# Retention with two expert layers on one core: weight loads spread over the attention chunks, and one more row buffer

## The chip, the cores and the metric

The kernel runs on one core of one Trainium2 chip. The time is the device time of one execution in microseconds (us); lower is better. The engines are TensorE (PE), VectorE (DVE), ScalarE (ACT), GpSimd (POOL) and SyncE (SP); SP, ACT and POOL each issue DMAs in their own order.

## What is computed

Four batches of 576 positions, eight heads of 64, go through retention (attention with a decay instead of a softmax). The 2304 rows of 512 go to one of eight experts each, and then through a layer that takes the maximum of three products.

```python
def _attn_ref(q, k, v):
    scores = scale * np.matmul(q, k.transpose(0, 1, 3, 2))
    gamma = 1.0 - 2.0 ** (-5.0 - np.arange(H, dtype=np.float32))
    rel = pos[:, None] - pos[None, :]
    Dmat = np.where(rel >= 0, gamma[:, None, None] ** rel[None, :, :], 0.0)
    return np.matmul(scores * Dmat[None, :, :, :], v)

def _moe_ref(x, w_gate, w1, w2, capacity):
    logits = x @ w_gate
    expert_idx = np.argmax(logits, axis=1)
    ...
    h = np.maximum(np.einsum('ecd,edf->ecf', disp, w1), 0.0)   # 8 x [512, 1024]
    y = np.einsum('ecf,efd->ecd', h, w2)                       # 8 x [1024, 512]
    ...                                                        # row i: gate_w[i] * y[its expert, its place]

def _moe2_ref(x, w1, w2, w3, w_out):
    h = np.maximum(np.maximum(x @ w1, x @ w2), x @ w3)
    return h @ w_out
```

All arrays are float32 (the last layer's weights are float64 in the input and are decoded in the kernel).

## The kernel before, in words

**Order.** The order on each engine is the order of the program. Engines wait for each other where tiles are written and read; a tile's buffer is given to a new tile when the old one's last reader is done. DMAs of SP and ACT stand in the queue of the engine that issues them, and an issue that has to wait stops what is queued behind it.

**Attention.** The loop runs over 20 chunks t of 128 rows (every fifth has 64). In the turn of chunk t, PE does the scores of chunk t+1 (L270), the transposes of chunk t-1 (L491), the update of the decayed state (L295) and the outputs of chunk t (L315, L327). DVE masks the scores (cut, L276), scales the outputs (L336) and the values (vprime, L254), and does the gate. Loads of qk run five chunks ahead and those of kv up to six; qk has five buffers and kv six. The table otab, with which DVE scales the outputs, is made in the first four turns: a spread multiplies the decay table decs by a selector and puts it on 128 partitions (L664).

**The gate** works on groups: chunks 0 to 4, 5 to 9 and 10 to 13. For a chunk in a group, take reduces the logits on DVE (L382), and then ACT copies the transposed rows from PSUM to a buffer xg (L389); the next transposes write the same PSUM tile. One turn after a group's last chunk, group_choose picks the experts (L408 to L415, gives goh); in the turn after that group_place counts on PE (gpo, L433, read by DVE at L443 as ghit), group_weigh finds weights and places, and group_send scales two chunks' rows a turn and stores them from xg to xd in HBM (L483, L484). Chunks from 14 on are done one by one by gate1 (L344 to L365), position (on PE, L497, into the same PSUM tile as gpo) and gate2. In chunk 18 POOL gathers the first expert's rows from xd (L174). The rows of the last three chunks are first set to zero in xd (L728) and added on PE.

**Weights of the experts.** Each expert has eight units of 128 x 1024 (four of w1, four of w2). load_unit brings one from HBM to raw (three buffers, SP). A split makes two parts of it: split_hi on ACT rounds it (L144), split_lo on DVE takes the rest (L149); split_lo frees raw. Units 0 to 7 have homes that are there from the start, those after them homes that come with the experts. In the attention loop units are loaded at LOAD_AT and split at SPLIT_AT, the DVE half one turn later, each followed there by another load; after the loop next_split splits one unit and loads the next.

**Experts.** Expert e does mm1 in eight steps f (a<-xt,w), each followed by ACT and DVE making h (L1113, L1114), and mm2 in four steps d (b<-h,w), each followed by ACT's copy to y (L1144). next_split stands after some steps. The last layer follows from some 420 us on and is not touched.

The names of the change: LOAD_AT, SPLIT_AT, ZERO_AT, the number of xg buffers, spread_otab with its selector sel, next_split's places in mm1 and mm2, and next_load.

Of the kernel before, what the change touches and what calls it, by code (L numbers as in the profile page):

```python
# [8 lines left out]
F32 = mybir.dt.float32  # L9
# [11 lines left out]
P = 128  # L21
B, H, S, D = 4, 8, 576, 64
DM = H * D
# [27 lines left out]
NPATCH = 3  # L51
LOAD_AT = [2, 4, 5]
SPLIT_AT = [4, 6, 7, 8, 9]
EARLY_SCATTER = 10
# [24 lines left out]
def retention_moe_max3_kernel(ctx: ExitStack, tc: tile.TileContext, qk, kv, consts, decay, tokid, cap, wg, wts, wts2, out):  # L79
# [81 lines left out]
    def next_load():  # L161
        if nxt["load"] < NUNIT:
            load_unit(nxt["load"])
            nxt["load"] += 1
# [33 lines left out]
    def attention():  # L198
        with ExitStack() as c2:
# [141 lines left out]
            def gate1(t):  # L341
# [25 lines left out]
                if NCHUNK - NPATCH <= t < NCHUNK - 1:  # L367
                    xg_t[t] = wk.tile([P, DM], F32, tag="xg", name=f"xg{t}", bufs=7)
                    act.activation(
                        out=xg_t[t][:L].rearrange("p (c n) -> p c n", c=NC), in_=xps_t[t][:L, :, :P], func=AF.Copy  # L370
                    )
# [7 lines left out]
            def take(t):  # L379
                L = CHUNKS[t][2]  # L380
                i = GROUP_OF[t]
                dve.tensor_reduce(  # L382
                    out=lgs[i % 2][:L, t - GROUPS[i][0]],
                    in_=xps_t[t][:L, :, P:].rearrange("p c e -> p e c"),
                    axis=AX.X,
                    op=ALU.add,
                )
                xg_t[t] = wk.tile([P, DM], F32, tag="xg", name=f"xg{t}", bufs=7)
                act.activation(  # L389
                    out=xg_t[t][:L].rearrange("p (c n) -> p c n", c=NC), in_=xps_t.pop(t)[:L, :, :P], func=AF.Copy  # L390
                )
# [114 lines left out]
            def gate2(t):  # L506
# [12 lines left out]
                xps = xps_t.pop(t)[:L, :, :P]  # L519
                xg = xg_t.pop(t) if t in xg_t else wk.tile([P, DM], F32, tag="xg", name=f"xg{t}", bufs=7)  # L520
                if t < NCHUNK - NPATCH:
# [135 lines left out]
            decs = st.tile([H, S], F32, name="decs")  # L657
            sel = st.tile([H, NPAIR, 2, D], F32, name="sel")

            def spread_otab(j):  # L660
                a, n = j * P, min(P, S - j * P)
                bank = ps_1.tile([P, DM], F32, tag="po", name=f"spread{j}")
                for r in range(NPAIR):
                    pe.matmul(  # L664
                        bank[:, r * n : (r + 1) * n], lhsT=sel[:, r].rearrange("h a d -> h (a d)"),
                        rhs=decs[:, a : a + n], start=True, stop=True,
                    )
                act.activation(
# [20 lines left out]
            for s_ in state:  # L689
# [11 lines left out]
            vprime(1)  # L701
            act.activation(
                out=sel,
                in_=ident[:H, :H].rearrange("h (r a) -> h r a", a=2).unsqueeze(3).to_broadcast([H, NPAIR, 2, D]),
                func=AF.Copy,
            )
            spread_otab(0)
# [9 lines left out]
            for t in range(NCHUNK):  # L717
# [3 lines left out]
                if t == 0:  # L721
                    act.dma_start(out=who_d.rearrange("(p c) o -> p (c o)", p=P), in_=zero)
                if t == 4:
                    tail = sum(L for _, _, L in CHUNKS[NCHUNK - NPATCH :])
# [73 lines left out]
                if t - 1 in SPLIT_AT:  # L798
                    split_lo(nxt["split"] - 1, dve)
                    if nxt["load"] < 8:  # L800
                        next_load()
                if t < NPOS - 1:
# [139 lines left out]
    with tc.manual_schedule():  # L942
# [158 lines left out]
        def mm1(e):  # L1101
            xt, wide = xt_t.pop(e), WIDTH[e]
            for f in range(F // P):
# [15 lines left out]
                if f % 2:  # L1119
                    units.pop(8 * e + f // 2)  # L1120
                if f % 2 or (e in (1, 3, 4) and f == 4):
                    if (e, f) != (0, 1):
                        next_split()
                dec_step(e, f)

        def mm2(e):
# [3 lines left out]
            for d in range(NC):  # L1130
# [14 lines left out]
                if e == E - 1:  # L1145
                    ysplit_part(0, d)
                next_split()
                dec_step(e, F // P + d)
# [70 lines left out]
        dec_load(1)  # L1219
        find_order()  # L1220
        load_x(1)
        for c in range(NC // 2):
# [559 lines left out]
```

## Time and profile before

| | |
|---|---|
| median of 3 runs | 668.2 us (661.24 to 670.61) |
| profiled execution | 665.12 us, its span 663.1 us |
| PE busy in the span | 634.7 us (96%) |
| DVE, ACT, POOL busy | 440.1, 277.2, 215.5 us |
| mean granted clock of PE | 0.984 |
| DMA | 124.05 MB, mean 187 GB/s |

Busy time of PE is that of matmuls, which are pipelined. The granted clock is a share of the full 2.4 GHz; 0.50 is 1.2 GHz. The idle time of an engine that nothing waits for costs nothing.

### The profile page before, as it was taken

Reading aid. Unit: us, or ns where it says so; the run is one execution under the profiler, and the core shown is the slowest. Engines: PE = TensorE matmul, PEld = TensorE weight load, DVE = VectorE, ACT = ScalarE, POOL = GpSimd, SP = SyncE. Lnnn points to the kernel's source line nnn. Section 1 sums busy time; section 2 is a strip of 40 time slices with the busy share of each in tenths; the row PEclk is TensorE's granted clock in tenths of the full one; section 3 lists DMA queues with packets and bytes.
Section 4 is the critical chain, followed back from the end, with each engine's and each line's share of the span. In section 5 each row is a group of like instructions: output and inputs, shape, how many; then the busy total and the mean of one; then the engine's idle time right before and its main releaser. Section 6 shows DMA issues by size and latency. Waiting matters only on the chain. (4 is left out here: it accounts for less than half of the span.)

```text
span 663.1 us, 12029 instructions
## 1 busy us (share of the span) xinstructions
PE 634.7 (96%) x4523; PEld 596.4 (90%) x4523; DVE 440.1 (66%) x869; ACT 277.2 (42%) x504; POOL 215.5 (33%) x188
## 2 busy tenths in 40 slices
PE   8999989899999999999989999999999999999995
PEld 5888877799999999898979999997899998999983
DVE  3478757774857578689697556577887677446630
ACT  2336324444656565555646543433522225221221
POOL 1001121255655745278885044540210002100011
PEclk8999968999999999999999999999999999999998
DMA  8889952255678787777866324357889641544011
GB/s 280 275 268 324 306 165 104 82 131 184 199 209 223 214 245 208 237 221 239 235 234 207 124 74 136 95 179 263 268 268 316 210 132 49 163 138 146 30 48 50
DMA packets 69876, 124.05 MB, mean 187 GB/s; under 512 B 18506, under 2 KB 41422, under 8 KB 69816
## 3 DMA queue, kind: packets, MB, share of 16 engines
q1 hardware_dynamic: 51896, 94.62, 45.8%
q0 software_dynamic: 15520, 24.50, 12.2%
q10 hardware_dynamic: 2400, 4.14, 1.8%
q8 instruction: 37, 0.61, 0.4%
q14 instruction: 23, 0.19, 0.1%
HBM read 97.27 MB, written 25.91 MB: 186 GB/s over the span
## 5 line engine op out<-in xcount | busy, mean ns | idle before, releaser
L149 DVE TENSOR_TENSOR w<-raw,w 128x1024 fp32r<-128x1024 f32 x72 | 99.9, 1389 | 44.7 <-ACT w L144 44.6
L1138 PE MATMUL b<-h,w 128*128 128x336 f32 (+7 forms) x768 | 118.5, 307 | 3.0 <-DVE h L1114 1.6
L1138 PEld LDWEIGHTS b<-h,w 128*128 128x128 f32 x768 | 109.0, 188 | 5.7 <-DVE h L1114 2.5
L144 ACT ACTIVATE w<-raw 128x1024 fp32r<-128x1024 f32 x72 | 75.9, 1055 | 25.4 <-DMA raw<-in_weights_dram 24.0
L1460 POOL DMA_INDIRECT out_dram<-o,perm_sb x18 | 20.0, 1110 | 192.2 <-ACT o L1458 160.0
L1098 PE MATMUL a<-xt,w 128*128 128x336 f32 (+7 forms) x256 | 77.6, 303 | 0.9 <-DVE xt L196 0.9
L1097 PE MATMUL a<-xt,w 128*128 128x336 f32 (+7 forms) x256 | 77.7, 304 | 0.0
L1099 PE MATMUL a<-xt,w 128*128 128x336 f32 (+7 forms) x256 | 77.3, 302 | 0.0
L187 POOL DMA_INDIRECT who_d<-tok,slots_i x20 | 22.7, 1135 | 100.3 <-DMA who_d<-tok,slots_i 62.2
L1098 PEld LDWEIGHTS a<-xt,w 128*128 128x128 f32 x256 | 48.2, 188 | 1.2 <-DVE xt L196 1.2
L1097 PEld LDWEIGHTS a<-xt,w 128*128 128x128 f32 x256 | 48.1, 188 | 0.5 <-ACT xt L195 0.5
L174 POOL DMA_INDIRECT xr<-xd,who x24 | 37.1, 1547 | 34.8 <-DVE order_w L1159 16.2
L1099 PEld LDWEIGHTS a<-xt,w 128*128 128x128 f32 x256 | 48.1, 188 | 0.0
L1494 PE MATMUL s<-b_ys,w 128*128 128x384 f32 x216 | 40.7, 335 | 1.6 <-ACT p L1524 1.6
L1097 PE MATMUL u<-ys,w 128*128 128x384 f32 x126 | 42.1, 334 | 0.0
L1098 PE MATMUL u<-ys,w 128*128 128x384 f32 x126 | 42.1, 334 | 0.0
L1099 PE MATMUL u<-ys,w 128*128 128x384 f32 x126 | 42.1, 334 | 0.0
L1494 PE MATMUL s<-b_xt,w 128*128 128x384 f32 x216 | 40.4, 334 | 0.0
L1494 PE MATMUL s<-b_h,w 128*128 128x384 f32 x216 | 40.3, 334 | 0.0
L1494 PEld LDWEIGHTS s<-b_ys,w 128*128 128x128 f32 x216 | 37.6, 188 | 2.2 <-ACT p L1524 1.9
L1113 ACT ACTIVATE h<-a 128x336 fp32r<-128x336 f32 (+7 forms) x64 | 26.6, 422 | 29.8 <-PE a L1099 29.6
L1494 PEld LDWEIGHTS s<-b_xt,w 128*128 128x128 f32 x216 | 37.8, 188 | 0.2
(287 smaller groups left out, 1329.1 us busy)
## 6 DMA issues: line engine op xcount, KB each, us to landing
raw<-in_weights_dram SPq DMA_DIRECT2D x64, 512.0 KB, 5.2
w<-sd SPq DMA_DIRECT2D x68, 256.0 KB, 4.1
kv<-in_kv_dram SPq DMA_DIRECT2D x16, 512.0 KB, 5.9
qk<-in_qk_dram SPq DMA_DIRECT2D x15, 512.0 KB, 7.3
d<-in_weights_dram POOLq DMA_DIRECT2D x14, 512.0 KB, 5.9
sd<-y SPq DMA_DIRECT2D x13, 512.0 KB, 3.2
wdec<-mag POOLq DMA_DIRECT2D x16, 256.0 KB, 3.8
raw<-wdec SPq DMA_DIRECT2D x8, 512.0 KB, 3.7
```

The costliest lines, as they stand in the source:

```text
L144: act.activation(out=t[:, 0], in_=raws[w], func=AF.Copy)
L149: engine.tensor_tensor(out=t[:, 1], in0=raws.pop(w), in1=t[:, 0].bitcast(F32), op=ALU.subtract)
L174: pool.indirect_dma_start(out=xr[:n, r, :], out_offset=None, in_=xd[:, :], in_offset=bass.IndirectOffsetOnAxis(ap=who[:n, r, e : e + 1] if ...
L187: pool.indirect_dma_start(out=who_d[:, :], out_offset=bass.IndirectOffsetOnAxis(ap=slots_i[:L, t : t + 1], axis=0), in_=tok[:L, t : t + 1] ...
L1097: pe.matmul(ps, lhsT=wh, rhs=xh, start=first, stop=False)
L1098: pe.matmul(ps, lhsT=wh, rhs=xl, start=False, stop=False)
L1099: pe.matmul(ps, lhsT=wl, rhs=xh, start=False, stop=last)
L1113: act.activation(out=h[:, 0, :wide], in_=ps, func=AF.Relu)
L1138: pe.matmul(ps, lhsT=w[:, a, f * P : (f + 1) * P], rhs=hs[f][:, b, :wide], start=(i == 0), stop=(i == len(todo) - 1),)
L1460: pool.indirect_dma_start(out=out[:, :], out_offset=bass.IndirectOffsetOnAxis(ap=perm_sb[:, g : g + 1], axis=0), in_=o, in_offset=None,)
L1494: pe.matmul(ps, lhsT=a[:, k], rhs=b[:, c], start=first and c == 0 and n == 0, stop=c == 1 and n == 2, skip_group_check=True,)
```

## The change

The loads of the eight units of the first expert are at eight chunks instead of at three plus one after each split, and all eight units are split in the attention loop instead of five. The zeros for the last rows of xd are stored in chunk 13 instead of chunk 4. xg has eight buffers instead of seven. The selector sel goes: the spread takes a column of the identity, broadcast to 64, as its stationary operand, in eight matmuls of 64 columns instead of four of 128. In the experts the places of the splits change, and three loads are issued ahead of the first expert.

```diff
-LOAD_AT = [2, 4, 5]
-SPLIT_AT = [4, 6, 7, 8, 9]
+LOAD_AT = [2, 3, 5, 6, 7, 10, 11, 12]
+SPLIT_AT = [4, 5, 8, 9, 10, 12, 13, 14]
+ZERO_AT = 13
...
-                    xg_t[t] = wk.tile([P, DM], F32, tag="xg", name=f"xg{t}", bufs=7)
+                    xg_t[t] = wk.tile([P, DM], F32, tag="xg", name=f"xg{t}", bufs=8)
...
-            sel = st.tile([H, NPAIR, 2, D], F32, name="sel")
...
                 for r in range(NPAIR):
-                    pe.matmul(
-                        bank[:, r * n : (r + 1) * n], lhsT=sel[:, r].rearrange("h a d -> h (a d)"),
-                        rhs=decs[:, a : a + n], start=True, stop=True,
-                    )
+                    for par in range(2):
+                        h = 2 * r + par
+                        pe.matmul(
+                            bank[par * D : par * D + D, r * n : (r + 1) * n],
+                            lhsT=ident[:H, h : h + 1].to_broadcast([H, D]),
+                            rhs=decs[:, a : a + n], start=True, stop=True,
+                        )
...
-            act.activation(
-                out=sel,
-                in_=ident[:H, :H].rearrange("h (r a) -> h r a", a=2).unsqueeze(3).to_broadcast([H, NPAIR, 2, D]),
-                func=AF.Copy,
-            )
...
-                if t == 4:
+                if t == ZERO_AT:
...
                 if t - 1 in SPLIT_AT:
                     split_lo(nxt["split"] - 1, dve)
-                    if nxt["load"] < 8:
-                        next_load()
...
-                if f % 2 or (e in (1, 3, 4) and f == 4):
-                    if (e, f) != (0, 1):
-                        next_split()
+                if f == F // P - 1 or (e and f % 2):
+                    next_split()
...
-                next_split()
+                for _ in range(2 if e in (1, 3) and d == NC - 1 else 1):
+                    next_split()
...
         find_order()
+        for _ in range(3):
+            next_load()
         load_x(1)
```

## Rows read from the trace of the kernel before

**Rows 1.** Windows: busy time by engine, granted clock, DMA share, GB/s; experts, then clock stretches.

```profile
133.24:476.00 342.76, 336.35 (x2184) 324.70 (x2184) 248.38 (x404) 177.13 (x302) 181.87 (x146) 1.00 0.65 196
...
10.68:14.09 3.41, 3.41 (x41) 2.94 (x38) 1.89 (x3) 0.83 (x3) 0.00 (x0) 0.50 1.10 375
85.77:96.01 10.24, 10.24 (x97) 9.28 (x98) 4.58 (x19) 2.24 (x8) 1.92 (x2) 0.50 0.55 172
106.25:109.66 3.41, 3.41 (x22) 2.96 (x18) 2.40 (x9) 2.13 (x3) 0.00 (x0) 0.50 0.39 150
109.66:133.24 23.58, 20.50 (x208) 17.88 (x207) 17.31 (x83) 9.91 (x27) 4.76 (x3) 1.00 0.26 81
```

**Rows 2.** PE in order of time: start, duration, line, tiles, count, idle before.

```profile
8.87 1.15 PE L664 MATMUL spread<-decs,sel 8*128 8x128 f32 x8 [1.07 <-ACT sel L702]
...
26.04 1.09 PE L327 MATMUL o<-pt,vp 128*64 128x128 f32 x16
...
58.31 1.19 PE L491 MATMUL xps<-idw,xT 128*128 128x136 f32 x8 [0.94 <-ACT xg L389]
...
69.57 0.17 PE L433 MATMUL gpo<-goh,tri 128*128 128x8 bf16 x1 [0.93 <-DVE goh L414]
...
85.03 1.51 PE L491 MATMUL xps<-idw,xT 128*128 128x136 f32 x8 [2.01 <-ACT xg L389]
...
97.63 0.16 PE L497 MATMUL po<-oh,tri 64*64 64x8 bf16 x1 [1.02 <-DVE ghit L443]
```

**Rows 3.** ACT in order of time.

```profile
8.19 0.63 ACT L702 ACTIVATE sel<-cst 8x512 f32<-8x512 f32 x1 [5.95 <-DMA cst<-in_consts_dram]
...
57.66 0.60 ACT L389 ACTIVATE xg<-xps 128x512 f32<-128x512 f32 x1 [0.99 <-DVE eq L476]
...
84.38 0.60 ACT L389 ACTIVATE xg<-xps 128x512 f32<-128x512 f32 x1 [3.94 <-DMA xd<-xg]
...
268.16 1.06 ACT L144 ACTIVATE w<-raw 128x1024 fp32r<-128x1024 f32 x1 [3.48 <-DMA raw<-in_weights_dram]
```

**Rows 4.** PE's waits in attention: sum in us, times, longest.

```profile
PE xps L491 <- ACT xg L389: 3.2, 3, 2.0
```

**Rows 5.** The SP queue in order of time: issues of DMAs.

```profile
31.77 3.04 SPq L728 DMA_DIRECT2D xd<-zero  x4
...
37.66 7.54 SPq L138 DMA_DIRECT2D raw<-in_weights_dram  x2
```

**Rows 6.** Windows, as in rows 1, at chunk 5.

```profile
42.00:46.00 4.00, 4.00 (x56) 3.52 (x55) 3.76 (x12) 1.24 (x4) 0.00 (x0) 1.00 0.28 79
```

**Rows 7.** DVE in order of time.

```profile
67.68 0.69 DVE L254 TENSOR_TENSOR vp<-kv,cat 128x512 f32<-128x512 f32 x1 [0.91 <-DMA kv<-in_kv_dram]
...
69.71 1.22 DVE L149 TENSOR_TENSOR w<-raw,w 128x1024 fp32r<-128x1024 f32 x1
...
91.53 0.18 DVE L408 TENSOR_REDUCE gmx<-lgs 128x4 f32<-128x32 f32 x1
...
92.75 0.22 DVE L415 TENSOR_TENSOR gids<-goh,tab 128x64 bf16<-128x64 bf16 x1
94.89 0.18 DVE L344 TENSOR_REDUCE lg<-xps 64x8 f32<-64x32 f32 x1 [1.91 <-PE xps L491]
...
97.41 0.17 DVE L443 TENSOR_TENSOR ghit<-gpo,goh 128x32 f32<-128x32 f32 x1
```

**Rows 8.** Waits of the SP queue in attention.

```profile
SPq L231 <- DMA xd<-xg: 8.6, 2, 6.5
```

**Rows 9.** Windows, as in rows 1, of chunks 13, 14 and 15.

```profile
77.70:81.86 4.16, 4.16 (x57) 3.78 (x55) 2.95 (x8) 2.32 (x5) 0.00 (x0) 1.00 0.98 377
81.86:90.60 8.74, 6.73 (x69) 5.93 (x67) 2.78 (x7) 2.56 (x5) 0.90 (x1) 0.72 1.03 332
90.60:98.46 7.86, 6.84 (x73) 6.08 (x73) 5.03 (x22) 1.58 (x6) 2.88 (x3) 0.66 0.09 16
```

**Rows 10.** PE's waits from 133 us on.

```profile
PE b L1138 <- ACT h L1113: 1.4, 2, 0.9
```

More of the change, by code (lines that the diff above doesn't have):

```diff
@@ L387, in take @@
                 )
-                xg_t[t] = wk.tile([P, DM], F32, tag="xg", name=f"xg{t}", bufs=7)
+                xg_t[t] = wk.tile([P, DM], F32, tag="xg", name=f"xg{t}", bufs=8)
                 act.activation(
@@ L519, in gate2 @@
                 xps = xps_t.pop(t)[:L, :, :P]
-                xg = xg_t.pop(t) if t in xg_t else wk.tile([P, DM], F32, tag="xg", name=f"xg{t}", bufs=7)
+                xg = xg_t.pop(t) if t in xg_t else wk.tile([P, DM], F32, tag="xg", name=f"xg{t}", bufs=8)
                 if t < NCHUNK - NPATCH:
```

## Prediction

> **What bounds the kernel now.** I read the windows over the experts, the stretches in which the granted clock is low, PE's waits, and then the single engines in order of time around each wait.
>
> TensorE (PE) is the bound. From 133 us on, where the first expert starts, up to 476 us it works 336.35 of 342.76 us at the full clock [rows 1]. Whatever the change does to ACT, DVE or the loads there can win 6.4 us at most. More can be won ahead of 133 us, in the twenty attention chunks, and it has two forms: waits of PE, and stretches at the lower clock (0.50, that is 1.2 of 2.4 GHz). There are three of these, of 3.41, 10.24 and 3.41 us [rows 1]. The middle one begins at 85.77 us, just after PE's longest wait, 2.01 us ahead of the transposes at 85.03 [rows 2]. At half rate 10.24 us do the work of 5.1, so this one event costs 2.0 + 5.1 = 7.1 us.
>
> Its cause: the transposes write the bank that ACT's copy to xg must first empty, and that copy starts at 84.38, after 3.94 us of waiting for a store xd<-xg [rows 3]. xg has seven buffers, so chunk 12's copy takes the buffer of chunk 5, whose store has not landed. I read the same wait at 57.66, where chunk 7 takes chunk 0's buffer, though the row names DVE as the releaser; PE's transposes wait 0.94 us behind it [rows 2, 3]. In PE's list these waits have the largest sum, 3.2 us [rows 4].
>
> **The change, part by part.** Sums go against the profiled execution, 665.1 us (a span of 663.1 and 2.0 around it). The median of the three runs, 668.2, is 3.1 above it and the runs lie between 661.2 and 670.6; the forecast is for a run like the profiled one, and the range has to hold the others.
>
> *sel goes.* Ahead of the first spread PE waits 1.07 us for ACT's copy sel, which takes 0.63 and itself waited for cst until 8.19 [rows 2, 3]. Now the spread reads cst: **-0.6**. Instead of four matmuls of 128 columns a spread has eight of 64, in two halves of the output. No row shows 8 rows by 64 columns. The nearest, o's sixteen records of 128*64, take 1.09 us against 1.15 for the eight of a spread [rows 2]: -0.3 for five spreads. If the halves run one after the other, each spread costs another 1.1, +5.5 in all. I take 0, since the nearer row has the same two halves.
>
> *The eighth xg buffer.* Chunk 7 gets a buffer of its own: **-0.9**. Chunk 12 takes chunk 4's, stored long before, and the 2.0 us go. Next in line is chunk 13, for chunk 5's buffer. Its copy would come near 85 us; that store had landed by 84.38 [rows 3], so I count no new wait.
>
> *Loads one by one, zeros later.* At chunk 5 the SP queue stood for 7.54 us at two raw loads, the second waiting for DVE's split of unit 0, with chunk 10's qk and kv queued behind [rows 5]; meanwhile the DMA engines fell to a share of 0.28 between 42 and 46 us [rows 6]. Now unit 3's load stands behind qk10 and kv10, and the zeros, 3.04 us of issuing, are out of chunk 4 [rows 5]. That brings a megabyte forward. What it can win is seen behind kv: DVE waits 0.91 us for one ahead of 67.68, and behind that PE waits 0.93 us for goh, ahead of 69.57 [rows 2, 7]. I take **-0.5**, between 0 and -0.9.
>
> Units 5, 6 and 7 now load in chunks 10, 11 and 12, and on SP the next chunk's qk and kv stand behind each. Each waits for the split of the unit three before it, which DVE does in the chunk ahead. The next qk has to wait for its own buffer, until outputs of the chunk in work has read it, so I set this to 0; where the split is late it is one split, 1.2 us, for each of three. The zeros stand in front of qk19 and kv19, which are needed in chunks 19 and 16, and ahead of the gather in chunk 18: 0, and 3.0 if kv had no such cover. SP also waits up to 6.5 us for an xd store whose data the kv load behind it has nothing to do with [rows 8]. Which load meets which store depends on the order, so this can win or lose some 3 us; I take 0.
>
> *Three more splits in attention.* Units 5, 6 and 7 were split in the first expert, under a PE that didn't wait. Now each takes ACT 1.06 us in chunks 12 to 14 [rows 3] and DVE 1.22 us in chunks 13 to 15 [rows 7]. In these three chunks DVE works 2.95, 2.78 and 5.03 us, PE 4.16, 6.73 and 6.84, the last two stretched by the low clock [rows 9]. With the splits DVE has 10.8 + 3.7 = 14.4 us; PE, without the 5.1, has 12.6. DVE is no longer the idle one. The tight spot is chunk 15, where PE may not write position's result before DVE has read ghit from the same bank: 1.02 us of waiting now, up to 97.63 [rows 2]. On DVE choose takes 1.44 us (91.53 to 92.97), and from gate1's start to ghit's end are 2.69 (94.89 to 97.58) [rows 7]; with a split between, 5.35. PE passes from choose's start to that wait in 5.08 us, 4.48 of it at half rate, so in 2.8 at full. It would then wait 2.5, that is 1.5 more than now. Unit 7's split next delays gate1 of chunk 16 by 1.2, for which PE waits as well. Of the 7.1 us there remain 2.0 + 5.1 - 1.5 - 1.2 = **4.4**, the largest term and the least certain.
>
> The clock has to stay up for that. It fell after the 2.01 us of waiting, and again at 106.25 after shorter waits, but not between 109.66 and 133.24, where PE is idle for 3.1 us in all [rows 1]. The Trainium skill (TensorE: Matmul & The Clock Gate, HAM oscillation) says that idle gaps between bursts of matmuls throttle the array, and that the ramp is paid anew after each. By that rule a new wait of 2.5 us in chunk 15 brings the low clock back, and the time is that of the second rival below. This trace agrees for the wait ahead of 85.03.
>
> *In the experts.* Unit 8's split moves to the first expert's last f, so splits run one unit ahead; the loads of units 8 to 10 move up, behind SP's wait for the order that DVE finds, with nothing urgent queued behind: 0. The extra split at f = 4 of experts 1, 3 and 4 goes, and a second one follows the last d of experts 1 and 3. Two waits of PE for h, 1.4 us together [rows 10], are in experts 3 and 4; ahead of 268.16 ACT stands 3.48 us at a raw load that has not landed, with h behind it [rows 3]. I take **-0.9**, between 0 and -1.4.
>
> Sum: 0.6 + 0.9 + 0.5 + 4.4 + 0.9 = 7.3; 665.1 - 7.3 = **657.8 us**.
>
> **The rivals.** *DVE keeps up.* DVE's waits take in the splits, PE's wait in chunk 15 stays as it is, and the two short low stretches, worth 1.7 us each, go as well: the first since PE's wait ahead of it shrinks from 1.07 to 0.4. For it: DVE was busy for 2.78 of the 8.74 us of chunk 14 [rows 9]. Against: choose, split and gate1 are one chain on one engine. 0.6 + 1.7 + 0.9 + 0.9 + 7.1 + 1.7 + 1.4 = 14.3, which gives 650.8.
>
> *The stall only moves.* PE waits 2.5 us in chunk 15 instead of 2.0 in chunk 14, and a low stretch as long as before follows there. Then the big term is 2.0 - 1.5 - 1.2, a loss of 0.7; the rest wins 2.9: 662.9. For it: a wait of that length was enough before. A buffer that does nothing, since stores land later still behind the three loads and the zeros, comes to the same time within a microsecond, and is counted here.
>
> *Slower: a second long low stretch.* As the last, and chunks 16 to 19, whose gate chain already stops PE in every chunk, stay at half rate for another 10.24 us: 662.9 + 5.1 = 668.0. [...] Against: the clock held from 109.66 on through similar waits [rows 1].
>
> **How the numbers follow.** Forecast 0.5, DVE keeps up 0.2, the stall moves 0.2, slower 0.1. The range from 651 to 668 holds the first and third and about half of each end, some 0.85; the +5.5 of the spreads, added to the forecast, is 663.3 and lies within. A measurement of this kernel tells about 2%, 13 us, from no change. Against the median of 668.2 that is 654.8: the second case and little of the first, 0.2. Slower by 2% would be 681.6, which no case reaches: 0.02. Within 2%: 0.78.
>
> **What would show it.** Right: the first spread starts near 8.2 us; ACT's copy to xg waits for no store; the transposes of chunk 13 follow the scores of chunk 15 at once; the clock is full between 82 and 90; PE's longest wait is now the one for ghit in chunk 15, 2 to 3 us; the first expert starts near 127 us. Wrong: a spread of over 1.5 us, SP at a raw load in chunks 10 to 12 with DVE waiting for kv, or a low stretch of 10 us after 88.

## The result

The change made the kernel slower by 1%: 670.08 us median of 20 runs against 662.52 us for the kernel before, a ratio of 1.010 (95% interval 1.0075 to 1.0126). The ratio leaves out slow runs (three of the 20 of after), and the profiled executions of c3 and g2 below are slow ones. The forecast was 657.8, with a range of 651 to 668. The loss stays within the 2% for which the prediction gave 0.78, but 670.08 lies 2.1 us above its range. The profiled execution of after took 671.97 us, its span 670.1 us.

The view first to be read is the windows over the four low stretches of the clock ahead of the first expert and over two parts of the experts, of after (columns as in [rows 1]):

```profile
10.59:14.00 3.41, 3.41 (x43) 3.12 (x40) 1.89 (x3) 0.76 (x2) 0.00 (x0) 0.50 1.10 360
92.51:99.34 6.83, 6.04 (x48) 5.14 (x49) 5.67 (x24) 2.13 (x3) 1.91 (x2) 0.50 0.44 109
109.58:112.99 3.41, 3.22 (x16) 3.24 (x17) 1.23 (x10) 0.22 (x2) 0.15 (x1) 0.50 0.20 77
119.82:123.23 3.41, 3.41 (x20) 2.94 (x17) 1.94 (x10) 0.73 (x2) 0.00 (x0) 0.50 0.26 90
130.66:254.56 123.90, 122.81 (x818) 120.75 (x818) 81.56 (x145) 62.48 (x108) 73.00 (x56) 1.00 0.72 204
254.56:289.99 35.43, 31.57 (x206) 29.31 (x205) 23.73 (x44) 16.55 (x29) 13.67 (x13) 0.95 0.69 203
```

The 10.24 us at half rate from 85.77 on [rows 1] are gone, but 6.83 us follow seven microseconds later. The first expert starts at 130.66 instead of 133.24, so 2.6 us are won ahead of it, where 6.4 were forecast. Then the time goes the other way. Expert 4, the last window, takes 35.43 us for 206 matmuls, with 3.41 us of it at half rate, from 276.83 on; before it took 30.50 us for as many, at the full clock:

```profile
257.53:288.03 30.50, 29.54 (x206) 27.79 (x205) 22.75 (x43) 16.88 (x29) 12.21 (x12) 1.00 0.73 224
```

At its end after is 2.0 us late, at the start of expert 7 4.8 (352.27 against 347.51), and at the end of the span 7.0. Expert 4 alone loses 4.9 us; expert 6 loses another 2.5 (32.33 us against 29.79), and what follows from expert 7 on 2.3.

PE in order of time, all of after:

```profile
8.42 1.09 PE L666 MATMUL spread<-decs,cst 8*64 8x128 f32 x16 [0.62 <-DMA decs<-in_decay_dram]
...
69.67 0.17 PE L434 MATMUL gpo<-goh,tri 128*128 128x8 bf16 x1 [2.11 <-DVE goh L415]
...
93.30 0.16 PE L498 MATMUL po<-oh,tri 64*64 64x8 bf16 x1 [2.56 <-DVE ghit L444]
...
269.44 3.25 PE L1133 MATMUL b<-h,w 128*128 128x296 f32 x20 [1.67 <-DVE h L1110]
273.41 0.77 PE L1133 MATMUL b<-h,w 128*128 128x296 f32 x2 [0.72 <-DVE h L1110]
275.65 0.78 PE L1133 MATMUL b<-h,w 128*128 128x296 f32 x2 [1.47 <-DVE h L1110]
```

Against [rows 2]: a spread takes 1.09 us as worked out and its wait fell from 1.07 to 0.62; the waits for ACT's copies to xg are gone; the wait for goh, which I had at 0.4, grew from 0.93 to 2.11; the wait for ghit is 2.56, forecast 2.5. The last three rows, in which expert 4 waits 3.9 us for h, stand against 1.4 us in experts 3 and 4 together before [rows 10]. What stands ahead of h is seen on ACT, which makes its first half:

```profile
255.14 1.05 ACT L145 ACTIVATE w<-raw 128x1024 fp32r<-128x1024 f32 x1
257.13 1.06 ACT L145 ACTIVATE w<-raw 128x1024 fp32r<-128x1024 f32 x1 [0.94 <-DMA raw<-in_weights_dram]
258.09 0.71 ACT L1109 ACTIVATE h<-a 128x296 fp32r<-128x296 f32 x2
265.63 1.06 ACT L145 ACTIVATE w<-raw 128x1024 fp32r<-128x1024 f32 x1 [6.84 <-DMA raw<-in_weights_dram]
```

The two splits behind the last d of expert 3 stand at 255.14 and 257.13. ACT then comes to a split whose raw load has not landed and stands there for 6.84 us, with the next h queued behind it. Before it stood 3.48 at that place [rows 3]. The trace has that load issued at 255.14 and landed at 265.61, 10.47 us later; the three loads of raw ahead of it whose landing the trace shows took 4.3 to 4.9. POOL's gather of expert 5's rows falls into the time of the slow one:

```profile
251.25 1.71 POOL L175 DMA_INDIRECT xr<-xd,who  x1 [0.31 <-issue]
253.26 1.66 POOL L175 DMA_INDIRECT xr<-xd,who  x1 [0.31 <-DVE step L1197]
255.23 0.92 POOL L175 DMA_INDIRECT xr<-xd,who  x1 [0.30 <-issue]
```

### The profile page after: what moved, and what is told of

Read it like the earlier page. It is cut to its first block, busy times and chain, and to the rows that moved or that the text cites. A ratio compares the mean times of both kernels' runs of the same rounds, so it can differ in the third digit from the quotient of the medians.

```text
span 670.1 us, 12114 instructions
## 1 busy us (share of the span) xinstructions
PE 637.6 (95%) x4563; PEld 597.8 (89%) x4563; DVE 437.9 (65%) x869; ACT 275.1 (41%) x503; POOL 211.0 (31%) x188
## 4 chain that ended last, share of the span: by engine, by line
PE 58%; DMA 12%; DVE 12%; issue 5%; POOL 5%; ACT 5%; SPq 0%; ACTq 0%; POOLq 0%; DVEq 0%
PE s L1492 19%; PE b L1133 9%; DMA raw<-in_weights_dram 4%; PE d L1476 3%; PE d L1478 3%; PE d L1477 3%; DVE w L150 3%; DMA wdec<-y 3%; PE a L1094 3%; PE a L1093 3%; PE a L1095 3%; PE xps L492 2%; PE o L328 2%; PE sc L271 2%; PE o L316 2%
## 5 line engine op out<-in xcount | busy, mean ns | idle before, releaser
L1133 PE MATMUL b<-h,w 128*128 128x336 f32 (+7 forms) x768 | 121.2, 310 | 6.7 <-DVE h L1110 5.7
L1133 PEld LDWEIGHTS b<-h,w 128*128 128x128 f32 x768 | 110.5, 190 | 10.6 <-DVE h L1110 7.8
L175 POOL DMA_INDIRECT xr<-xd,who x24 | 35.6, 1482 | 33.3 <-DVE order_w L1155 17.7
L1037 POOL TENSOR_TENSOR d<-d,top 128x512 f32<-128x512 f32 x16 | 21.4, 1335 | 56.2 <-ACT h L1109 19.2
```

Of the source, the lines that this page charges most:

```text
L175: pool.indirect_dma_start(out=xr[:n, r, :], out_offset=None, in_=xd[:, :], in_offset=bass.IndirectOffsetOnAxis(ap=who[:n, r, e : e + 1] if ...
L1037: pool.tensor_tensor(out=low, in0=low, in1=top.bitcast(F32), op=ALU.mult)
L1133: pe.matmul(ps, lhsT=w[:, a, f * P : (f + 1) * P], rhs=hs[f][:, b, :wide], start=(i == 0), stop=(i == len(todo) - 1),)
```

## The experiments

A ratio is that of a variant to the kernel before, measured beside it on one chip; differences of ratios are not measured side by side. "The rest" is the time from the first expert's matmuls to the end of the span, in a profiled execution. One lesson came early: two more profiles of the unchanged kernel before had the first expert at 127.47 and 132.82, so a single start says little; waits and the rest say more.

### The places of the splits in the experts

**The old places in the changed kernel** (a1_experts_back).

```diff
-                if f == F // P - 1 or (e and f % 2):
+                if e and (f % 2 or (e in (1, 3, 4) and f == 4)):
                     next_split()
...
-                for _ in range(2 if e in (1, 3) and d == NC - 1 else 1):
-                    next_split()
+                next_split()
```

> The changed kernel with the places of the splits in the experts as in the kernel before (no split at the first expert's last f; an extra one at f = 4 of experts 1, 3 and 4; one after each d). Theory 1, the extra split behind expert 3's last d costs the time: experts 4 to 6 lose the 4.9 to 7.4 us that the trace of the changed kernel shows there, attention keeps its 2.6 us of gain, so 660 to 665, at or under the kernel before. Theory 2, the experts lose since attention ends earlier and their loads meet the gathers by chance: as slow as the changed kernel, 668 to 671.

665.46 us, ratio 1.0035 (1.0003 to 1.0067). The places account for 1.010 less 1.0035, some 4.3 us, with an interval of about 2.7 either way. Some 2 us of loss remain.

**Only expert 3's second split back at f = 4** (a2_e3_at_f4).

```diff
-                if f == F // P - 1 or (e and f % 2):
+                if f == F // P - 1 or (e and f % 2) or (e == 3 and f == 4):
...
-                for _ in range(2 if e in (1, 3) and d == NC - 1 else 1):
+                for _ in range(2 if e == 1 and d == NC - 1 else 1):
```

> The changed kernel with one split moved: the second one behind expert 3's last d goes back to f = 4 of expert 3. Theory 1: ACT's wait of 6.8 us for a raw load at the start of expert 4 goes, mm1 and mm2 of expert 4 get back their 4.9 us, about 665. Theory 2: no change, about 670.

664.1 us, ratio 1.0041 (1.0013 to 1.0069), which can't be told from a1: this one place does nearly all of it.

**The double split put into the kernel before** (b1_double_at_e3): expert 4's extra split moves to a second one behind expert 3's last d.

```diff
-                if f % 2 or (e in (1, 3, 4) and f == 4):
+                if f % 2 or (e in (1, 3) and f == 4):
...
-                next_split()
+                for _ in range(2 if e == 3 and d == NC - 1 else 1):
+                    next_split()
```

> The kernel before with one split moved: the extra one at f = 4 of expert 4 is done a step group earlier, as a second split behind the last d of expert 3. Theory 1: slower than before by about 5 us (667 where before is 662). Theory 2: as before, within 1 us.

666.26 us, ratio 1.0053 (1.0025 to 1.0081), 3.5 us, with nothing else of the change in it.

**Without the gather of expert 5** (a4_no_gather5). It leaves out the gather of expert 5's rows, and expert 5 works on those of expert 4.

```diff
+        if e == 5:
+            xr_t[e] = xr_t[e - 1]
+            return
         xr = xpool.tile([P, NR, DM], F32, tag="xr", name=f"xr{e}")[:RP]
```

> The changed kernel without the gather of the rows of the sixth expert (number 5), which runs while expert 4 begins; that expert works on the rows of expert 4 instead, so this part of the output is another one. If the gather is what makes the raw load land late behind the two splits, ACT's wait of 6.8 us at the start of expert 4 falls below 2 and the time falls by about 5 us, to 665. If the two splits alone use up the three raw buffers, whatever the gather does, the wait stays above 5 and the time at 670.

ACT at its longest wait for a raw load early in expert 4, one row each of a1, a2, b1 and a4 (ACT in order of time):

```profile
263.29 1.06 ACT L145 ACTIVATE w<-raw 128x1024 fp32r<-128x1024 f32 x1 [3.63 <-DMA raw<-in_weights_dram]
```
```profile
266.08 1.06 ACT L145 ACTIVATE w<-raw 128x1024 fp32r<-128x1024 f32 x1 [4.17 <-DMA raw<-in_weights_dram]
```
```profile
265.69 1.06 ACT L144 ACTIVATE w<-raw 128x1024 fp32r<-128x1024 f32 x1 [6.02 <-DMA raw<-in_weights_dram]
```
```profile
252.80 1.06 ACT L145 ACTIVATE w<-raw 128x1024 fp32r<-128x1024 f32 x1 [0.98 <-DMA raw<-in_weights_dram]
```

With the old place the wait is 3.6 and 4.2 (3.48 in before), with the double split 5.7 to 6.8 (5.73 in c2, the second profile of after), without the gather under 1. So two things together make it: a load that lands late beside the gather, as before's of 9.5 and 10.2 us do too, and a double split that brings ACT to it earlier. Expert 4 as a whole takes 35.0 to 35.6 us in the three profiles with both (after, c2, b1), 28.5 in a4, and 29.0 to 32.7 in the sixteen others.

The time of the last variant did not follow, 667.57 us and a ratio of 1.011 (1.0057 to 1.0164) from four runs. In its profile it reaches expert 7 8.7 us earlier than before, and its last matmul 4.5 us earlier (11.1 earlier than after). But then 14.1 us pass to the end of the span, where the nineteen other profiles have 8.2 to 8.7: POOL's closing DRAIN takes 6.03 us, 1.38 in after. So the total says little about the gather; why the DRAIN is longer stays open. The 4.2 us lost in the last layer sent me to the rest of the kernel.

**An extra split where no engine waits** (d2_extra_in_e2).

```diff
-                if f % 2 or (e in (1, 3, 4) and f == 4):
+                if f % 2 or (e in (1, 2, 3) and f == 4):
```

> The kernel before with one place moved: the extra split at f = 4 of expert 4 is done at f = 4 of expert 2. If it is the raw load beside the gather in experts 3 and 4 that costs the time (the theory from the three variants of the experts), an expert 2 in which no engine waits takes the split for nothing, and expert 4 has one split less: the wait of ACT for a raw load there falls under 3 us, and the time is 0 to 2 us under before (ratio 0.997 to 1.000). Rival: any move of a split by one step shifts the loads into the gather and costs 3 us (ratio 1.004 or more), as the move from f = 4 of expert 4 to the end of expert 3 did.

662.64 us, ratio 1.0031 (0.9982 to 1.0079), which settles neither. ACT's wait in expert 4 stayed at 4.42, so my reason for a gain was wrong, and a new wait of PE of 1.36 us stands ahead of the next transposes (220.99): expert 2 was not free.

### Ahead of the experts

**Spread and eighth buffer alone** (b4_spread_xg8): the kernel before with the new spread_otab as in the change, and

```diff
-            sel = st.tile([H, NPAIR, 2, D], F32, name="sel")
...
-                xg_t[t] = wk.tile([P, DM], F32, tag="xg", name=f"xg{t}", bufs=7)
+                xg_t[t] = wk.tile([P, DM], F32, tag="xg", name=f"xg{t}", bufs=8)
```

> The kernel before with two parts of the change alone: the spread without sel, and eight xg buffers. Theory 1, that of the prediction (the waits for sel and for the xd store, and the long low stretch behind the second, are all that these parts touch): the experts start 6 to 8 us earlier than in the profile of before, near 126, the low stretch at 86 is gone, and with the placing of splits unchanged the time falls by 5 us or more, a ratio under 0.993. Theory 2 (the start of the experts moves by some 3 us between executions of one program, and what is won ahead of them is partly given back to weight loads in the experts and to the store ahead of the last layer's second part): the store waits are gone as well, but the time falls by 0 to 3 us, a ratio of 0.995 to 1.000. Theory 3 (the spread in two halves costs more than it wins): a ratio above 1.

663.97 us, ratio 1.0018 (0.9976 to 1.0059). The first expert starts at 125.82, the earliest of all, and the end of the span, 662.1, is only 1.0 earlier than before. Theory 2 came nearest, and theory 3 is not excluded; but the waits that I called the store's were not there in every execution of before either, as the next shows.

**The kernel before, twice more** (c1_before_again, c3_before_third), unchanged.

> The kernel before, unchanged, for a second profile. Theory 2 of the first run (executions of one program differ in attention): the experts start 1 to 4 us earlier than the 133.24 of the first profile, and the low stretch at 86 is shorter than 10.24. Theory 1: within 1 us of 133.24, and 10.24 us again.

> The kernel before once more, for a third profile. From the two there are, the experts start at 127 to 133 us and the rest takes 529 to 530 us after that. If the rest takes 534 or more in this one, the longer rest of the variants (535.7 to 536.5) is a matter of executions; if it takes 529 to 531, it belongs to the variants.

c1 took 658.53 us, c3 668.04. PE ahead of the transposes of chunk 13, and the ten microseconds that were at half rate in the first profile; c1, then c3:

```profile
82.93 1.19 PE L491 MATMUL xps<-idw,xT 128*128 128x136 f32 x8 [0.23 <-ACT xg L389]
...
91.48 0.16 PE L497 MATMUL po<-oh,tri 64*64 64x8 bf16 x1 [1.44 <-DVE ghit L443]
```
```profile
85.38:95.62 10.24, 8.80 (x137) 7.73 (x137) 8.26 (x39) 2.93 (x9) 1.92 (x2) 1.00 0.50 128
```
```profile
84.58 1.45 PE L491 MATMUL xps<-idw,xT 128*128 128x136 f32 x8 [2.37 <-ACT xg L389]
```
```profile
85.38:95.62 10.24, 10.24 (x97) 9.28 (x97) 4.68 (x19) 2.36 (x8) 1.92 (x2) 0.50 0.56 175
```

The stall on which my largest term rested is a property of the execution. Over eight profiles of kernels with seven buffers and before's loads, PE's wait at this place was 0.23, 1.09, 1.25, 1.40, 1.78, 2.01, 2.35 and 2.37 us; the last three, and they alone, were followed by 10.24 us at half rate there. And with the clock up, PE's wait for ghit in chunk 15 is 1.44 already in c1; the 1.02 of [rows 2] was so short because PE came at half rate (of the eight, the three at half rate have 0.79 to 1.02, the five others 1.44).

**The changed kernel again** (c2_after_again), unchanged.

> The changed kernel, unchanged, for a second profile. If the loss is the raw load behind the gather in expert 4, ACT waits 5 to 7 us for a raw load near 260 again and expert 5 starts 4 to 5 us later against expert 4 than in before. If that was one execution's accident, the wait is under 3 us.

671.47 us; first expert at 129.17, the wait for ghit 2.56 again, 6.83 us of low clock from 91.03, ACT 5.7 us at a raw load, expert 5 at 289.12. No accident.

**Eighth buffer alone** (f3_xg8_old_spread): bufs=8, with sel standing in the first of the eight.

```diff
-            sel = st.tile([H, NPAIR, 2, D], F32, name="sel")
+            sel = wk.tile([P, DM], F32, tag="xg", name="sel", bufs=8)[:H].rearrange("h (r a d) -> h r a d", r=NPAIR, a=2)
```

> The kernel before with eight xg buffers and the spread with sel, which stands in the first of the eight until chunk 7 takes it. Theory of the prediction for this part: the waits of ACT for xd stores at chunks 7 and 12 are gone, and the long low stretch at 86 with them where an execution has it, so the experts start at 126 to 128. If the eighth buffer makes the rest longer, the rest is 535 to 539 and the time 661 to 665; if not, 529 to 533 and the time 656 to 660, 1 to 3 us under before.

662.46 us, ratio 1.001 (0.9967 to 1.0053). Both store waits are gone, as forecast, and the only wait of PE for a copy to xg is 0.28 us. The first expert starts at 128.49 in spite of 10.24 us at half rate from 11.51 on, which is ahead of everything that the buffer touches. No gain that this measurement can tell; the forecast was 1 to 3 us under before.

**Loads one by one and zeros at chunk 13 alone** (f4_loads).

```diff
-LOAD_AT = [2, 4, 5]
-SPLIT_AT = [4, 6, 7, 8, 9]
+LOAD_AT = [2, 3, 5, 6, 7, 10, 11, 12]
+SPLIT_AT = [4, 5, 8, 9, 10]
...
-                if t == 4:
+                if t == 13:
...
-                    if nxt["load"] < 8:
-                        next_load()
```

> The kernel before with the loads one by one at the eight chunks and the zeros at chunk 13, the splits of units 0 to 4 where the change has them, and everything else as before. My prediction for this part was 0.5 us won ahead of the choice of the second group. If that holds, PE's wait for goh is under 0.5 us. Rival (kv waits for the landing of an xd store on the same semaphore, and the bytes in flight are the same): that wait stays at 0.9 to 2.1 us, the waits for xd stores at chunks 7 and 12 stay, and the time is 0 to 3 us above before, the two groups of variants (0.2 per cent over before without these loads, 0.4 with them) differing by this.

662.02 us, ratio 0.9997 (0.9962 to 1.0031). PE's wait for goh is 0.99 and DVE's for kv ahead of it 0.96, against 0.93 and 0.91 in [rows 2, 7]. A gain of 0.5 us is not seen; but PE's wait there is 1.55 in c1 and under 0.2 in c3, both before unchanged, so one profile can't settle half a microsecond.

**All of the attention part but the three extra splits** (b6_attn5): the changed kernel with the old places in the experts, and

```diff
-SPLIT_AT = [4, 5, 8, 9, 10, 12, 13, 14]
+SPLIT_AT = [4, 5, 8, 9, 10]
...
-        for _ in range(3):
-            next_load()
```

> The changed kernel with only five units split in the attention loop (units 5 to 7 split in the first expert) and all the places in the experts as before; the loads one by one, the zeros at chunk 13, eight buffers and the new spread stay. Theory 1 (the three extra splits delay gate1 and ghit on DVE): the wait for ghit in chunk 15 goes from 2.56 back to about 1.0 us, the low stretch at 92 goes with it, and the time is 2 to 4 us below the variant with the places as before and eight splits in attention (665.5), so 661.5 to 663.5. Rival (the wait comes from the loads and stores): the wait of 2.56 stays, and the time is 665 to 666.

665.38 us, ratio 1.0044 (1.0009 to 1.0079). PE's rows for ghit, here and with eight splits (a1):

```profile
89.36 0.16 PE L498 MATMUL po<-oh,tri 64*64 64x8 bf16 x1 [1.45 <-DVE ghit L444]
```
```profile
92.27 0.16 PE L498 MATMUL po<-oh,tri 64*64 64x8 bf16 x1 [2.56 <-DVE ghit L444]
```

The extra splits add 1.1 us to this wait, as theory 1 has it, and with them a low stretch follows at 91 to 93 us. The total doesn't tell the two kernels apart; the 2 to 4 us forecast are not seen.

**Splits and loads later** (d3_late_loads), an edit of b4.

```diff
-SPLIT_AT = [4, 6, 7, 8, 9]
+SPLIT_AT = [4, 6, 11, 12, 13]
```

> The kernel before with the spread without sel, eight xg buffers, and the splits of units 2, 3 and 4 in chunks 11 to 13 instead of 7 to 9, so that the loads of units 4 to 7 leave chunks 7 to 10 and go to chunks 7 and 12 to 14, where the stores are done. Theory (between 50 and 90 us the DMA engines are full, so the wait of DVE for a kv load ahead of the choice of the second group, and PE's wait for goh behind it, come from the bytes in flight): the kv wait there falls from 2.1 to under 0.7 us and PE's wait for goh from 1.7 to under 0.5; the experts start 1 to 2 us earlier than in the variant with spread and eighth buffer alone (125.8 in its profile), and the time is 661 to 664. Rival (kv waits for a store on the same semaphore, whatever the bytes): the two waits stay within 0.5 us of 2.1 and 1.7, and the time is that of that variant, 664.

670.16 us, ratio 1.0145 (1.0095 to 1.0196). PE and DVE:

```profile
68.11 0.17 PE L433 MATMUL gpo<-goh,tri 128*128 128x8 bf16 x1 [2.08 <-DVE goh L414]
...
91.19 0.16 PE L497 MATMUL po<-oh,tri 64*64 64x8 bf16 x1 [2.56 <-DVE ghit L443]
```
```profile
66.22 0.69 DVE L254 TENSOR_TENSOR vp<-kv,cat 128x512 f32<-128x512 f32 x1 [2.05 <-DMA kv<-in_kv_dram]
```

The wait for kv stays at 2.05, but the edit did not empty the DMA engines: their share between 50 and 90 us is 0.98, as in b4. So the theory of full engines is neither borne out nor refuted. The splits in chunks 12 to 14 make ghit late again, and the gate chunks then run 10.24 us at half rate, from 118.63 on. That is a part of the loss; I did not take the rest of it apart.

### The rest of the kernel, which nobody edited

> The kernel before with the spread without sel and eight xg buffers once more, for a second profile. The first had the experts at 125.8 us and 536.3 us for the rest. If the longer rest belongs to the program, 534 to 538 again; if to the execution, 529 to 532 is as likely. The experts start near 126 again if the two waits that the parts remove are what sets the start, and anywhere between 125 and 131 if not.

**c4_spread_xg8_again**, b4 unchanged, took 671.84 us; its first expert starts at 130.58 and its rest is 539.4. So the longer rest belongs to the program. b3, f2 and f3 (above) then asked which part brings it.

**The spread alone** (b3_spread), and **the spread with ACT still making sel** (f2_spread_keep_sel), which nobody reads. In both:

```diff
-                    pe.matmul(
-                        bank[:, r * n : (r + 1) * n], lhsT=sel[:, r].rearrange("h a d -> h (a d)"),
...
+                    for par in range(2):
+                        h = 2 * r + par
```

> The kernel before with the spread without sel alone, seven xg buffers. In three profiles of before the work from the first expert on took 529.1 to 533.3 us; in the two of the variant with spread and eighth buffer 536.3 and 539.4, though none of it was edited. If the spread (fewer instructions of ACT, more of PE ahead of the experts) makes the rest longer, the rest is 535 to 539 here too and the time 662 to 665; if the eighth buffer does, the rest is 529 to 533 and the time within 1 us of before.

> As the one above, but ACT still makes sel, which nobody reads, so that memory and ACT's instructions are those of before and only PE's matmuls of the spread change. If the rest of that one is 535 or more and this one's 529 to 533, the longer rest hangs on ACT's instructions or the memory; if both are long, on PE's; if both are short, on the eighth buffer.

666.05 us, ratio 1.0073 (1.003 to 1.0116), and 667.26 us, 1.0091 (1.0048 to 1.0135). The part that I had booked as a small gain costs 4.8 us in b3 and 6.0 in f2, so with either memory layout, and the eighth buffer alone (f3) costs nothing that can be told. PE's two places of the last layer, c1 and then f2:

```profile
444.71 0.50 PE L1478 MATMUL d<-w,h 128*128 128x512 f32 x1 [0.61 <-ACT h L1284]
...
471.95 1.31 PE L1494 MATMUL s<-b_ys,w 128*128 128x384 f32 x6 [1.53 <-ACT p L1524]
```
```profile
448.73 0.50 PE L1481 MATMUL d<-w,h 128*128 128x512 f32 x1 [1.82 <-ACT h L1287]
...
477.70 1.34 PE L1497 MATMUL s<-b_ys,w 128*128 128x384 f32 x6 [3.27 <-ACT p L1527]
```

What the spread adds to the program is 40 matmuls with their weight loads, 80 instructions of PE; the trace of before has 9,171 of PE. The page's list of DMA queues has instruction blocks on q8, packets of 16 KB (c1, then f2):

```profile
q8 instruction: 37, 0.61, 0.4%
```
```profile
q8 instruction: 38, 0.62, 0.4%
```

All seven profiles of kernels with before's number of PE instructions have 37 such packets, all thirteen with more have 38, so I take q8 for PE's. 9,171 instructions in 37 packets are some 250 a packet, an estimate, so 80 more ahead of all else move every later fetch forward against the work. The trace has the packets at 9.3, 30.4 and 52.8 us after the first expert's start in before, and at 3.7, 22.5 and 43.7 in b4. (The 3.5 that the expectation of g1 below names for before is not in the trace.)

**80 instructions without the spread** (g1_rows80), and **176 more with it** (g2_spread_xg8_rows176), 256 in all.

```diff
-            def warm(n):
+            def warm(n, c=DM, m=P):
...
-                    pe.matmul(w, lhsT=one[:, :P], rhs=one, start=True, stop=True)
+                    pe.matmul(w[:m, :c], lhsT=one[:, :m], rhs=one[:, :c], start=True, stop=True)
...
-            warm(9)
+            warm(49, 94, 32)
```

In g2 it is warm(97, 48, 32), on top of b4.

> The kernel before, with the nine warming matmuls of 512 columns at its start as 49 of 94 columns: 40 matmuls, 80 instructions of PE, more ahead of everything, as many as the new spread adds, and no other work. Theory (the places in time at which PE's instruction blocks of 16 KB are fetched move 80 of 256 instructions, some 7 us, earlier against the work, and a fetch that falls into a piece's load of the last layer makes it land 1.5 us late): the fetches stand where the spread's variants have them, 3.5 to 3.8, 22.5 and 43.5 us after the first expert's start (before: 3.5, 9.3, 30.4), the last load of such a piece takes 6.0 to 6.2 us instead of 4.4, PE waits 1.8 us in the last layer's first down instead of 0.6, the rest is 534 to 538 and the ratio 1.005 to 1.009. Rival (the spread itself does it): the wait is 0.3 to 0.8 as in before, the rest 529 to 533, the ratio 0.997 to 1.003.

> The new spread and eight xg buffers, and the warming matmuls as 97 of 48 columns: 88 matmuls, 176 instructions more, so that with the 80 of the spread the blocks lie as in before, one block later. Theory: the wait in down is 0.3 to 0.8 again, the rest 529 to 533 instead of 536 to 539, the time 657 to 661 and below the variant without them (664), ratio 0.993 to 0.999. Rival (the spread or the buffer does it): the wait of 1.8 stays, the rest is 535 to 539, the ratio 1.002 to 1.008.

g1: 672.67 us, ratio 1.0126 (1.0058 to 1.0193) from four runs. g2: 664.61 us, ratio 0.9984 (0.9939 to 1.0029); its profiled execution took 669.19. The packets are at 3.6, 22.6 and 43.5 in g1, and at 9.3, 29.3 and 52.7 in g2, as meant. PE's rows, g1 and then g2:

```profile
456.93 0.50 PE L1478 MATMUL d<-w,h 128*128 128x512 f32 x1 [0.26 <-ACT h L1284]
...
486.04 2.29 PE L1494 MATMUL s<-b_ys,w 128*128 128x384 f32 x6 [3.44 <-ACT p L1524]
```
```profile
454.90 0.50 PE L1475 MATMUL d<-w,h 128*128 128x512 f32 x1 [0.50 <-ACT h L1281]
...
482.19 1.32 PE L1491 MATMUL s<-b_ys,w 128*128 128x384 f32 x6 [1.57 <-ACT p L1521]
```

| kernel | first expert | the rest | wait in down | wait for p |
|---|---|---|---|---|
| before, three profiles | 133.24, 127.47, 132.82 | 529.9, 529.1, 533.3 | 0.60, 0.61, 0.31 | 1.57, 1.53, 1.63 |
| f3, eighth buffer | 128.49 | 532.7 | 0.73 | 1.60 |
| f4, loads | 128.40 | 533.7 | 1.06 | 1.80 |
| g2, spread, buffer, 256 instructions | 134.36 | 533.0 | 0.50 | 1.57 |
| b3, spread | 133.69 | 534.6 | 1.78 | 1.48 |
| f2, spread, sel kept | 127.41 | 536.4 | 1.82 | 3.27 |
| b4 and again, spread and buffer | 125.82, 130.58 | 536.3, 539.4 | 1.85, 1.83 | none, 1.64 |
| b6, attention part, five splits | 127.63 | 535.7 | none | 2.95 |
| a1, attention part | 127.91 | 536.5 | 0.49 | 3.19 |
| g1, 80 instructions | 131.65 | 541.1 | 0.26 | 3.44 |

The four upper lines, whose blocks lie as in before, have a rest of 529.1 to 533.7 and short waits at both places. The lower ones have 534.6 to 541.1 and a long wait at one place or both. The seven profiles that the table leaves out sort the same way at these two places: b1 and d2, with before's count, have waits of at most 0.8 and 1.6, and a2, a4, c2, d3 and after have a long one each. (b1's rest is 536.0, with 35.6 us in expert 4.)

80 instructions that do no work of the spread reproduce the loss in g1's time. That 176 more take the long waits away again rests on one profile of g2, since its time, 0.9984, can't be told from b4's 1.0018. So a larger count of PE's instructions is shown as a cause; that the places of their blocks decide is borne out by the way all twenty profiles sort, and not shown more directly. One thing besides the count differs in g1 and g2: from 11 and 12 us on they have 10.24 us at half rate, where before has 0 or 3.41. Whether the smaller warming matmuls bring that is not shown (f3 has it too, with the old ones). It can be a part of g1's 1.0126, but not of its longer rest.

How the count acts is shown in part. In g1 some eight of the eleven us by which its rest is longer than in the first profile of before lie in the experts, ahead of both places in the table, and three behind. Expert 6 takes 29.1 to 30.8 us in the eight profiles with the blocks of before, and 31.1 to 33.3 in the eleven others that gather expert 5's rows; this is after's second loss. In nine of these eleven PE waits 0.4 to 2.1 us for gathered rows there, in the eight 0.33 at most (c1, then g1):

```profile
328.56 0.50 PE L972 MATMUL tp<-cst,xr 118*128 118x118 f32 x2 [0.33 <-DMA xr<-xd,who]
```
```profile
340.14 0.52 PE L972 MATMUL tp<-cst,xr 118*128 118x118 f32 x2 [1.78 <-DMA xr<-xd,who]
```

In the last layer, eight loads a profile bring pieces of its weights. Behind the second of each eight ACT is still busy with the first; of the other 140, seven are slow: ACT's operation behind them begins 6.0 to 6.3 us after the issue, against 3.7 to 5.7 elsewhere. Each of the seven has a q8 packet 2.8 to 3.8 us after its issue. In five of them it is the eighth load, and these are the five profiles with a wait of 1.8 us in down (after, b3, b4, c4, f2). But three other loads have such a packet too and take 4.3 to 4.6. One is g1's eighth: the wait in down that was forecast for g1 is 0.26 us, and its long one is that for p. What makes ACT late for p in g1 (it waits for a store of the output there), and what lengthens g1's expert 3 to 33.3 us (30.4 in before), I did not settle.

## Why the prediction was wrong

**sel goes, -0.6.** The 0 for the two halves was right, 1.09 us a spread. The wait fell from 1.07 to 0.62, now for the load of decs; but in c1 the same wait for sel is 0.31, so a single pair of profiles does not measure it. The step that failed is the term itself: it holds the wait and the time that the spreads take, and puts at nothing what 80 more instructions do to PE's program behind them, without a reason. Measured on its own the part is not -0.6 but a ratio of 1.0073 (1.003 to 1.0116), +4.8 us.

**The experts' places, -0.9.** Wrong sign; measured +4.3 as a difference of two ratios, and +3.5 when the double split alone is put into before (ratio 1.0053, 1.0025 to 1.0081). I had the row in hand, ACT 3.48 us at a late raw load with h behind it [rows 3], and took the moved split as relief because two waits of PE were near the old place. I did not ask when the raw buffer of the moved split's successor is issued and what else is on the queues then: the gather.

**The chunk 14 stall, -4.4.** Mechanism right, size wrong. The wait for ghit came out at 2.56 for 2.5, and the waits for stores went. But 2.0 + 5.1 us were booked from one execution; of three profiles of before, two have that stall and one has 0.23 and full clock. The second rival's mechanism, a low stretch behind the new wait, came true: 6.83 us in both profiles of after, 3.41 in a1, a2 and a4. The rule that I weighed, that gaps between bursts of matmuls throttle the array (Trainium skill, TensorE: Matmul & The Clock Gate, HAM oscillation), agrees with these rows. But the length of a wait does not decide (the section's own case is one of longer waits): of PE's waits for goh, 1.55 us in c1 and 1.67 in b4 were followed by 3.41 us at half rate within 1.4 us, and 2.07 to 2.20 in after, c2, c4 and d3 by none for 20 us and more. Averaged over five profiles with before's attention loop unedited (before, b1, c1, c3, d2: 133.24, 129.96, 127.47, 132.82, 130.16) the first expert starts at 130.7, over five with after's (after, c2, a1, a2, a4: 130.66, 129.17, 127.91, 129.21, 125.87) at 128.6: some 2.2 us won, not 6.4, with starts that lie up to 5.8 us apart among the first five.

**Loads one by one, -0.5.** No gain that can be told: 0.9997 (0.9962 to 1.0031).

**The slower rival** ended at 668 through a second low stretch in chunks 16 to 19. The time came out there, and for other reasons; none of my cases let work behind 133 us become longer than it was, since PE had only 6.4 us of idle time there to win. That bound holds for gains only.

Chained, against 662.5: spread 1.0073, with the buffer 1.0018, with loads and zeros 1.0044, with three more splits 1.0035, with the experts' places 1.010, so about +4.8, -3.6, +1.7, -0.6 and +4.3 us. Each step has an interval of some 3 to 4 us either way, and only the first and the last are clear of it. No variant beat the kernel before; f4, g2, f3, b4 and d2 can't be told from it.

## What to carry to other kernels

Take a second and a third profile before a stall is made the largest term of a sum: here the same program lost 7 us in one execution and nothing in the next. A split or load that is moved by one step must be followed to the next load that it delays or meets, with the gather on the other queue beside it. And where a kernel is at 96% of one engine, count the instructions that an edit adds to that engine's program, since all that stands behind them is fetched at other moments.

## What I had not expected of the hardware

80 more instructions of PE at the start of the program, beside 9,171, moved the time by 1.3% (g1); in its profile the first expert starts at 131.65 us, within the range of before, and the rest takes 541.1 us, in before 529.1 to 533.3. A wait of 1.78 us left the clock up at the transposes of chunk 13 and one of 2.01 was followed by 10.24 us at half rate. Yet waits of 2.07 to 2.20 us for goh left the clock up in four profiles, so the length of a wait alone does not tell. And the early low stretch, from 10 to 12 us on, is 0 or 3.41 us long in executions of one program (before and after); 10.24 us stand there in f3, g1 and g2 alone.
